# Attention and two feed-forward layers in one kernel: half-column weight loads, a rewritten opening order, and products of zeros

## The chip, the cores and the metric

The kernel runs on one core of a Trainium2 chip. A core has a matrix engine (TensorE, PE in the rows, its weight loads PEld), a vector engine (VectorE, DVE), a scalar engine (ScalarE, ACT), a general engine (GpSimd, POOL), and a queue engine that issues the transfers here (SyncE, SP). Each executes its own instructions in order. The metric is the device time of one execution in microseconds.

## The reference, cut to what matters

```
x = causal_attention(q, k, v)         # 2 batches x 12 heads, 448 tokens, width 64 -> 896 x 768
h = ((x @ w1) * (x @ w2)) @ w3        # 768 -> 1024 -> 1024
y = h @ w_out                         # 1024 -> 768
z = relu(y @ w_in2) ** 2 @ w_out2     # 768 -> 2048 -> 768
```

q, k and v are float32. The weights arrive as 8-byte floats. Softmax subtracts the row maximum and divides by the row sum plus 1e-9.

## The kernel before, in words

**Attention and one weight product share the opening.** The 24 heads go in 12 pairs p. While VectorE and ScalarE do softmax, TensorE has time left, and it fills it with the product w3 @ w_out (into `wraw`), so that h @ w_out needs one product less later. That product is cut into 32 units `(g, i, n)`: group g of four w_out tiles, tile i of w3, column half n (384 columns). `fill()` issues none, one or two units at a time by a fixed count. The loop has 13 slots; slot p does the softmax of pair p and the values of pair p - 1.

**One pair's work.** `scores(p)`: TensorE, four row blocks (112 to 448 columns wide) for each of two heads, into six PSUM banks. `minima(p)`: VectorE adds the mask and takes the row extremum, block by block, which also frees the six banks. `exps(p, j)`: ScalarE, head j. `divide(p, j)`: two small VectorE instructions that wait for the exponentials, then four multiplications, on GpSimd, or on VectorE for head 1 of pairs 0, 1 and 11. `p_transposes(h)`: ten TensorE transposes into three banks of the same six, and three ScalarE copies out (L277). `attend(p)`: the product with v, into one of two banks that the units use too. `x_parts(p)`: ScalarE and VectorE write the two parts of the result.

**Weights.** A weight tile goes through three stages, in a fixed list `order`. Load (L78): 128 x 768 or 128 x 512 eight-byte words. Decode to float32: ScalarE L102, VectorE L103 and L108. Split into a high and a low part: ScalarE L90, VectorE L106. `step()` decodes the next tile of `order` and splits the next one of `parts`, and issues the loads that come free. At most two decoded tiles outside the plain ones wait for their split (`XB`); with two waiting, a step decodes nothing. The first two w3 tiles and the first four w_out tiles are also used as plain float32 (`PLAIN`): units of w3 tiles 0 and 1 are eight instructions of plain float32, all others twelve of split parts, and those need the split w3 tile and all four split w_out tiles of the group. Each unit is then copied out of its bank (L318, VectorE).

**What sets the order.** Inside `manual_schedule` the instructions of the engines named (TensorE, VectorE, ScalarE) run in the order in which the Python code writes them. Transfers and GpSimd are placed by a planner. An instruction waits for what it reads and for the buffers that it overwrites; the rest of its queue waits behind it. Slots 0 to 3 and 12 have an order of their own, slots 4 to 11 share one. A unit's place against the steps in a slot is thus a matter of the written order. `warm()` issues 36 transposes that nothing uses, ahead of the first real transposes. After the 13 slots come the four big products, in which TensorE is busy throughout.

Slot 3 before, with pair 2's values (steps in the order written):

```
scores(3); step(); minima(3); exps(3, 0); fill(); divide(3, 0)
p_transposes(4); p_transposes(5); step(); exps(3, 1); fill()
attend(2); divide(3, 1); x_parts(2); step(); fill()
```

Of the kernel before, what the change touches and what calls it, by code (L numbers as in the profile page):

```python
# [17 lines left out]
def attention_moe_moe2(ctx: ExitStack, tc: tile.TileContext, qk, v, w1, w2, w3, w_out, w_in2, w_out2, out):  # L18
# [13 lines left out]
    nc = tc.nc  # L32
# [17 lines left out]
    XB = 2  # L50
    RAW = 3
    PLAIN = 2
    WARM = 36
    NEAR = 2
    CLOSE = 4
# [13 lines left out]
        return nc.tensor.matmul(o, l, r, start=start, stop=stop)  # L69


    raws, f32s = {}, {}

    def load(key, src):
        n = src.shape[-1]
        pool, tag = (ringp, "ring") if key in LENT else (rawp, "raw")
        t = pool.tile([P, DM, 2], U32, tag=tag, name=f"raw_{key[0]}_{key[1]}")
        nc.sync.dma_start(out=t[:, :n].rearrange("p f w -> p (f w)"), in_=src.bitcast(U32))  # L78
        raws[key] = t[:, :n]

    def convert(a=None, b=None):

        if b:
            nm, n = b
            if nm == "w3":
                t = w3_tile(n)
            else:
                t = ringp.tile([P, 2, DM], F32R, tag="ring", name=f"hl_{nm}_{n}")
            x = wraw[:, n, :] if nm == "W" else f32s[b] if whole(b) else f32s.pop(b)
            nc.scalar.copy(t[:, 0], x)  # L90
            hls[b] = t
        if a:
            raw = raws.pop(a)
            n = raw.shape[1]
            low, high = raw[:, :, 0], raw[:, :, 1]
            if whole(a) and a[0] == "w3":
                y = w3_tile(a[1])[:, 0].bitcast(F32)
            elif whole(a):
                y = w3p[0].tile([P, DM], F32, tag="xw", name=f"xw_{a[1]}", bufs=NB)
# [4 lines left out]
            f32s[a] = y  # L104
# [28 lines left out]
    for g in range(N3 // KF):  # L133
        for i in range(KF):
            order += [("w3", g * KF + i)]
            if g == 0 and i == 0:
                order += [("wout", f) for f in range(NB)]
            if g == 0 and NB - 1 <= i < 2 * NB - 1:
                order += [("wout", i + 1)]
    order += ring[KF:]  # L140
    source = {"wout": w_out, "w1": w1, "w2": w2, "w3": w3, "win2": w_in2, "wout2": w_out2}
    place = {key: i for i, key in enumerate(order)}
# [36 lines left out]
    with (  # L179
# [2 lines left out]
        tc.tile_pool(name="attc", bufs=1) as attc,  # L182
        tc.tile_pool(name="ps_a", bufs=6, space=PSUM) as ps_a,
    ):
        ident = attc.tile([P, P], F32, tag="ident", name="ident")
        mask = attc.tile([CP, S], F32, tag="mask", name="mask")
        make_identity(nc, ident)
# [7 lines left out]

        def load_pair(p):
            t = attq.tile([P, 2, S], F32, tag="qk", name=f"qk{p}", bufs=3)
            nc.sync.dma_start(out=t.rearrange("p i s -> p (i s)"), in_=qk[p])
# [10 lines left out]
        def scores(p):  # L209

            y = qk_t.pop(p)
            st_t[p] = att.tile([CP, 4, 2, NCH], F32, tag="st", name=f"st{p}", bufs=3)
            ps = {}
            for j in range(2):
                p_t[2 * p + j] = att.tile([CP, off[NCH]], F32, tag="p", name=f"p{p}_{j}", bufs=4)
                for g in BLOCKS:
                    t = ps_a.tile([P, S], F32, tag="a", name=f"s{p}_{j}_{g[0]}")
                    o = 0
                    for i in g:
                        ps[j, i] = t[:CP, o:o + (i + 1) * CP]  # L220
                        o += (i + 1) * CP
            for g in BLOCKS:
                for i in g:
                    w = (i + 1) * CP
                    for j in range(2):
                        own = slice(j * D, (j + 1) * D)
                        mm(ps[j, i], y[own, 0, i * CP:w], y[own, 1, :w], True, True)
            s_t[p] = ps

        def blocks(p, j):  # L230
            return [(i, p_t[2 * p + j][:, off[i]:off[i + 1]]) for g in BLOCKS for i in g]

        def minima(p):

# [22 lines left out]
        def warm():  # L257

            t = ps_w.tile([P, HN], F32, tag="w", name="warm")
            for _ in range(WARM):  # L260
                nc.tensor.transpose(t[:CP, :CP], ident[:CP, :CP], ident[:CP, :CP])

        coff = [0, 4 * CP, 7 * CP, 9 * CP]

# [36 lines left out]
        def w_half(g, i, n):  # L301
# [12 lines left out]
            dst = wraw[:, i, cols]  # L314
            if g > 0:
                nc.vector.tensor_tensor(dst, acc, dst, op=ALU.add)
            else:
                nc.vector.tensor_copy(dst, acc)  # L318

        units = [(g, i, n) for g in range(N3 // KF) for i in range(KF) for n in range(2)]  # L320
        NU = len(units)


        parts = [key for key in order if not (key[0] == "w3" and key[1] < PLAIN)]
        steps = [0, 0]

        def free(key):

            if key[0] == "w3":
                return done[1] >= 2 * (key[1] - 1)  # L330
            k = in_ring.get(key, 0) - RING
            return k < 0 or k < NB and done[1] >= NU // 2

        def ahead(n):

            last = max(order.index(key) for key in LENT)
            return max(n + RAW, min(n + RAW + len(LENT), last + 1 + RAW))

        def step(f32=True, split=True):
            a, b = order[steps[0]], parts[steps[1]]  # L340
# [19 lines left out]
                done[1] += 1  # L360

        ET = mybir.EngineType
        with tc.manual_schedule(engines={ET.PE, ET.DVE, ET.Activation}):
            load_pair(0)
            load_pair(1)
            make_loads(2)
            load_v(0)
            make_loads(RAW)
            for p in range(SLOTS):
                softmax, attn_v = p < NP_ALL, p > 0  # L370
                if CLOSE <= p < NP_ALL:
                    load_v(p)
                    if p + 1 < NP_ALL:
                        load_pair(p + 1)
                    scores(p)
                    minima(p)
                    exps(p, 0)
                    fill()
# [9 lines left out]
                        step()  # L388
                    attend(p - 1)
                    x_parts(p - 1)  # L390
                    continue
                if softmax:
                    if p > 0:
                        load_v(p)
                        if p + 1 < NP_ALL:
                            load_pair(p + 1)
                        if p == 1:
                            make_loads(ahead(0))
                    scores(p)
                if p > 2:  # L400
                    step()
                if softmax:
                    minima(p)
                    if p == 1:
                        divide(0, 1)
                        step(split=False)
                    exps(p, 0)
                    if p < 2:
                        divide(p, 0)
                    if p < 3:  # L410
                        step(split=False)
                fill()
                if softmax and p > 1:
                    divide(p, 0)
                if attn_v:
                    if p == 1:
                        warm()
                    p_transposes(2 * (p - 1))
                    p_transposes(2 * (p - 1) + 1)
                    step(split=p > 1)  # L420
                if softmax:
                    exps(p, 1)
                fill()
                if p == 2:
                    step()
                if attn_v:
                    attend(p - 1)
                    if softmax and p > 1:
                        divide(p, 1)
                    x_parts(p - 1)  # L430
                    for _ in range(2 if p == 2 else 1):
                        step(split=p > 1)
                    if p == 1:
                        divide(1, 1)
                fill()
        assert not units and all(k in hls for k in ring[:KF])
        made.update(f32=steps[0], hl=steps[1] + PLAIN)
        for f in range(KF):
            used(("wout", f))

# [172 lines left out]
```

## Time and profile before

| what | us |
|---|---|
| median of 3 runs | 577.47 (577.46 to 577.71) |
| the profiled execution | 577.6 |
| its span, first to last instruction | 575.4 |
| TensorE busy in the span | 563.9 |
| TensorE's first product starts | 4.07 |
| end of the 13 slots (first product of the next stage) | 163.22 |

Times in rows count from the start of the span. The profiled execution is 2.2 us longer than its span, for what lies around it. A TensorE instruction's duration includes its way through the array, so neighbours overlap; from start to start is what one costs in a stream. The same holds for ScalarE and VectorE rows, whose successor often starts before the row's end.

### The profile page before, as it was taken

Reading aid. Unit: us, or ns where it says so; the run is one execution under the profiler, and the core shown is the slowest. Engines: PE = TensorE matmul, PEld = TensorE weight load, DVE = VectorE, ACT = ScalarE, POOL = GpSimd, SP = SyncE. Lnnn points to the kernel's source line nnn. Section 1 sums busy time; section 2 is a strip of 40 time slices with the busy share of each in tenths; the row PEclk is TensorE's granted clock in tenths of the full one; section 3 lists DMA queues with packets and bytes.
Section 4 is the critical chain, followed back from the end, with each engine's and each line's share of the span. In section 5 each row is a group of like instructions: output and inputs, shape, how many; then the busy total and the mean of one; then the engine's idle time right before and its main releaser. Section 6 shows DMA issues by size and latency. Waiting matters only on the chain.

```text
span 575.4 us, 8129 instructions
## 1 busy us (share of the span) xinstructions
PE 563.9 (98%) x3144; PEld 506.5 (88%) x3144; DVE 281.3 (49%) x567; ACT 268.2 (47%) x574; POOL 159.1 (28%) x140
## 2 busy tenths in 40 slices
PE   7899999999999999999999999999999999999997
PEld 5557777778989999999999999999999999999997
DVE  5987887767687544222210484555102854421011
ACT  5778777757865533222210456666002666640000
POOL 3367677776200312111100003333000023330000
PEclk9999999999999999999999999999999999999999
DMA  8854554233266633000000274333100763000111
GB/s 318 288 194 140 177 159 159 84 124 120 88 225 245 204 120 107 9 1 1 1 1 0 67 271 156 109 111 110 56 1 4 270 219 110 1 1 29 56 55 56
DMA packets 14823, 63.96 MB, mean 111 GB/s; under 512 B 1665, under 2 KB 1921, under 8 KB 14785
## 3 DMA queue, kind: packets, MB, share of 16 engines
q1 hardware_dynamic: 14784, 63.45, 32.2%
q8 instruction: 25, 0.41, 0.3%
q14 instruction: 14, 0.11, 0.1%
HBM read 60.69 MB, written 2.75 MB: 110 GB/s over the span
## 4 chain that ended last, share of the span: by engine, by line
PE 86%; DVE 6%; ACT 5%; issue 1%; DMA 1%; DVEq 0%; ACTq 0%
PE w L69 28%; PE g L69 20%; PE o L69 20%; PE h L69 10%; PE s L69 3%; PE x L69 2%; PE pp L273 2%; ACT p L245 2%; ACT pt L277 2%; DVE p L238 1%; DVE xw L108 1%; DMA qk<-in_qk 1%; ACT hl_wout L90 1%; DVE raw_wout L103 0%; DVE x_wout L108 0%
## 5 line engine op out<-in xcount | busy, mean ns | idle before, releaser
L69 PE MATMUL g<-hT,hl_win 128*128 128x448 f32 x576 | 117.2, 365 | 0.0
L69 PE MATMUL w<-xT,hl_w 128*128 128x448 f32 x576 | 117.0, 365 | 0.0
L69 PE MATMUL o<-hl_wout,gT 128*128 128x384 f32 x672 | 116.9, 334 | 0.0
L69 PEld LDWEIGHTS o<-hl_wout,gT 128*128 128x128 f32 x672 | 116.6, 188 | 0.1
L69 PEld LDWEIGHTS g<-hT,hl_win 128*128 128x128 f32 x576 | 108.1, 188 | 8.5
L69 PEld LDWEIGHTS w<-xT,hl_w 128*128 128x128 f32 x576 | 108.1, 188 | 8.5
L255 POOL TENSOR_SCALAR p<-p,st 112x448 f32<-112x448 f32 (+1 forms) x84 | 96.5, 1166 | 51.9 <-DVE st L252 23.3
L120 POOL TENSOR_TENSOR gT<-r,gT 128x448 fp32r<-128x448 f32 x32 | 39.1, 1245 | 195.8 <-ACT gT L119 128.7
L69 PE MATMUL w<-hl_wout,w 128*128 128x384 f32 x336 | 64.4, 342 | 0.5 <-DVE w L106 0.3
L245 ACT ACTIVATE p<-p,st 112x448 f32<-112x448 f32 (+1 forms) x96 | 49.7, 530 | 27.1 <-DVE st L238 27.0
L69 PEld LDWEIGHTS w<-hl_wout,w 128*128 128x128 f32 x336 | 57.4, 188 | 3.9 <-issue 0.9
L69 PE MATMUL h<-abT,hl_W 128*128 128x448 f32 x288 | 58.5, 365 | 0.0
L69 PEld LDWEIGHTS h<-abT,hl_W 128*128 128x128 f32 x288 | 54.1, 188 | 4.3
L120 POOL TENSOR_TENSOR abT<-a,abT 128x448 fp32r<-128x448 f32 x16 | 21.8, 1377 | 111.8 <-ACT abT L119 111.8
L238 DVE CUSTOM_DVE_ANT_0 p<-s,mask 112x448 f32<-112x448 f32 (+1 forms) x96 | 36.5, 441 | 7.0 <-PE s L69 7.0
L106 DVE TENSOR_TENSOR hl_wout<-x_wout,hl_wout 128x768 fp32r<-128x768 f32 x20 | 19.1, 957 | 37.9 <-ACT hl_wout L90 37.9
L533 ACT ACTIVATE r<-g 128x448 f32<-128x448 f32 x32 | 15.8, 542 | 40.8 <-PE g L69 40.8
L69 PE MATMUL s<-qk 64*112 64x448 f32 (+3 forms) x192 | 28.6, 443 | 4.1 <-DMA qk<-in_qk 4.1
L560 DVE TENSOR_TENSOR acc<-o,acc 128x384 f32<-128x384 f32 x14 | 7.2, 553 | 49.0 <-PE o L69 49.0
L273 PE MATMUL pp<-ident,p 112*112 112x112 f32 x240 | 27.9, 262 | 3.3 <-DVE st L238 1.6
L102 ACT ACTIVATE x_w<-raw_w 128x768 f32<-128x768 f32 (+1 forms) x30 | 24.4, 815 | 13.7 <-DVE hl_w L106 10.9
L273 PEld LDWEIGHTS pp<-ident,p 112*112 112x112 f32 x240 | 23.5, 134 | 8.0 <-issue 2.8
(62 smaller groups left out, 538.0 us busy)
## 6 DMA issues: line engine op xcount, KB each, us to landing
raw_wout<-in_w_out SPq DMA_DIRECT2D x24, 768.0 KB, 4.5
raw_w<-in_w SPq DMA_DIRECT2D x16, 768.0 KB, 4.3
raw_win<-in_w_in SPq DMA_DIRECT2D x16, 768.0 KB, 4.2
raw_w<-in_w SPq DMA_DIRECT2D x16, 512.0 KB, 3.9
qk<-in_qk SPq DMA_DIRECT2D x12, 448.0 KB, 5.1
v<-in_v SPq DMA_DIRECT2D x12, 224.0 KB, 2.6
out<-acc SPq DMA_DIRECT2D x6, 384.0 KB, 2.3
out<-acc SPq DMA_DIRECT2D x2, 192.0 KB, 1.8
```

What stands on the lines that cost most here:

```text
L69: return nc.tensor.matmul(o, l, r, start=start, stop=stop)
L90: nc.scalar.copy(t[:, 0], x)
L102: nc.scalar.activation(y, high.bitcast(F32), AF.Prelu, scale=2.0 ** -112, alpha=-2.0 ** 32)
L106: nc.vector.tensor_tensor(t[:, 1], x, t[:, 0].bitcast(F32), op=ALU.subtract)
L120: (engine or nc.vector).tensor_tensor(lo, x, hi.bitcast(F32), op=ALU.subtract)
L238: nc.vector.tensor_tensor_reduce(e, ps[j, i], mask[:, S - (i + 1) * CP:], QS, 3.0e38, ALU.add, ALU.min, st_t[p][:, 0, j, i:i + 1],)
L245: nc.scalar.activation(e, e, AF.Exp, bias=st_t[p][:, 0, j, i:i + 1], scale=-1.0, accum_out=st_t[p][:, 1, j, i:i + 1])
L255: engine.tensor_scalar(e, e, st[:, 3, i:i + 1], None, ALU.mult)
L273: nc.tensor.transpose(x[:CP, o:o + CP], pt[:, off[i] + c * CP:off[i] + (c + 1) * CP], ident[:CP, :CP],)
L277: nc.scalar.copy(t[:, coff[g[0]]:coff[g[0]] + o], x[:CP, :o])
L533: nc.scalar.activation(r, o[b], AF.Relu)
L560: nc.vector.tensor_tensor(a, o[n], a, op=ALU.add)
```

## The change

1. The first four w_out tiles are loaded and decoded in two column halves each: order now begins w3 0, w_out 0 to 3 (left half), w3 1, w_out 0 to 3 (right half), w3 2, w3 3, w3 4, w_out 4, w3 5, w_out 5 and so on. Units 1 and 2 change places, so that the first two units, (0, 0, 0) and (0, 1, 0), read left halves alone.
2. The four units of plain float32 are copied out by ScalarE (L318) in place of VectorE.
3. Slots 0 to 3 are written in another order, with four more steps in all; pair 0's blocks go from small to large, and its q and k come in two halves. Slots 4 to 12 keep their order. The transfers of the opening are issued in the written order too (SP joins the engines named).
4. TensorE begins with 8 products of a 112 x 112 tile of zeros (`warm_zeros`), which nothing uses. `warm()` stays.

Slot 3 after: `scores(3); step(); minima(3); exps(3, 0); fill(); divide(3, 0); p_transposes(4); p_transposes(5); step(); step(); exps(3, 1); fill(); attend(2); divide(3, 1); x_parts(2); step(); step(); fill()`.

```diff
+    WARM0 = 8
...
     def load(key, src):
-        n = src.shape[-1]
-        pool, tag = (ringp, "ring") if key in LENT else (rawp, "raw")
-        t = pool.tile([P, DM, 2], U32, tag=tag, name=f"raw_{key[0]}_{key[1]}")
-        nc.sync.dma_start(out=t[:, :n].rearrange("p f w -> p (f w)"), in_=src.bitcast(U32))
-        raws[key] = t[:, :n]
+        whole_key = key[:2]
+        if whole_key not in raw_t:
+            pool, tag = (ringp, "ring") if whole_key in LENT else (rawp, "raw")
+            raw_t[whole_key] = pool.tile([P, DM, 2], U32, tag=tag, name=f"raw_{key[0]}_{key[1]}")
+        cols = columns(key, src.shape[-1])
+        t = raw_t[whole_key][:, cols]
+        nc.sync.dma_start(out=t.rearrange("p f w -> p (f w)"),
+                          in_=src.bitcast(U32)[:, 2 * cols.start:2 * cols.stop])
+        raws[key] = t
+
+    def columns(key, n):
+
+        return slice(key[2] * n // 2, (key[2] + 1) * n // 2) if key[2:] else slice(0, n)
...
-            if g == 0 and i == 0:
-                order += [("wout", f) for f in range(NB)]
-            if g == 0 and NB - 1 <= i < 2 * NB - 1:
-                order += [("wout", i + 1)]
+            if g == 0 and i < 2:
+                order += [("wout", f, i) for f in range(NB)]
+            if g == 0 and NB <= i < 2 * NB:
+                order += [("wout", i)]
...
+        zeros = attc.tile([CP, CP], F32, tag="xw", name="zeros", bufs=NB)
+        nc.vector.memset(zeros, 0.0)
...
+            if p == 0:
+                x = qk[p].rearrange("p (i s) -> p i s", i=2)
+                for half in (slice(0, S // 2), slice(S // 2, S)):
+                    nc.sync.dma_start(out=t[:, :, half], in_=x[:, :, half])
...
-            for g in BLOCKS:
+            for g in BLOCKS if p else BLOCKS[::-1]:
...
+        def warm_zeros():
+
+            t = ps_w.tile([P, HN], F32, tag="w", name="warm0")
+            for _ in range(WARM0):
+                mm(t[:CP, :CP], zeros, zeros, True, True)
...
+            elif n3 < PLAIN:
+                nc.scalar.copy(dst, acc)
             else:
                 nc.vector.tensor_copy(dst, acc)
...
+        units[1], units[2] = units[2], units[1]
...
-        with tc.manual_schedule(engines={ET.PE, ET.DVE, ET.Activation}):
+        with tc.manual_schedule(engines={ET.PE, ET.DVE, ET.Activation, ET.SP}):
...
+                elif p == 1:
+                    minima(1)
+                    divide(0, 1)
+                    step(split=False)
+                    exps(1, 0)
+                    divide(1, 0)
+                    step(split=False)
+                    fill()
+                    warm()
+                    p_transposes(0)
+                    p_transposes(1)
+                    step(split=False)
+                    exps(1, 1)
+                    fill()
+                    attend(0)
+                    x_parts(0)
+                    step(split=False)
+                    divide(1, 1)
+                    fill()
+                elif p == 2:
+                    minima(2)
+                    exps(2, 0)
+                    divide(2, 0)
+                    step(split=False)
+                    fill()
+                    step(split=False)
+                    step(split=False)
+                    p_transposes(2)
+                    p_transposes(3)
+                    step(split=False)
+                    step(split=False)
+                    exps(2, 1)
+                    fill()
+                    attend(1)
+                    divide(2, 1)
+                    x_parts(1)
+                    step()
+                    step()
+                    fill()
...
+                    p_transposes(2 * (p - 1))
+                    p_transposes(2 * (p - 1) + 1)
+                    for _ in range(2 if p < CLOSE else 1):
+                        step()
+                    if softmax:
+                        exps(p, 1)
+                    fill()
```

## Rows read from the trace of the kernel before

**Rows 1.** The page, busy time and 40 slices of the granted clock (tenths).

```profile
PE 563.9 (98%) x3144; PEld 506.5 (88%) x3144; DVE 281.3 (49%) x567; ACT 268.2 (47%) x574; POOL 159.1 (28%) x140
...
PEclk9999999999999999999999999999999999999999
```

**Rows 2.** Busy time, 11 to 15 us: PE, PEld, DVE, ACT, POOL; granted clock.

```profile
11.00:15.00 4.00, 4.00 (x43) 3.89 (x42) 3.97 (x19) 4.00 (x16) 3.60 (x4) 1.00 1.01 413
```

**Rows 3.** Timeline of TensorE: start, length, what, count, idle before and its releaser.

```profile
4.07 7.07 PE L69 MATMUL s<-qk 64*112 64x448 f32 x32 [4.07 <-DMA qk<-in_qk]
...
14.57 1.16 PE L273 MATMUL pp<-ident,p 112*112 112x112 f32 x10
...
25.93 2.82 PE L273 MATMUL pp<-ident,p 112*112 112x112 f32 x20 [1.24 <-DVE st L238]
...
33.58 2.85 PE L69 MATMUL w<-xw,w 128*128 128x384 f32 x8 [0.20 <-DVE wraw L318]
36.35 2.15 PE L69 MATMUL s<-qk 64*112 64x448 f32 x16
...
41.12 2.81 PE L273 MATMUL pp<-ident,p 112*112 112x112 f32 x20
43.70 2.35 PE L69 MATMUL w<-hl_wout,w 128*128 128x384 f32 x12
45.98 2.11 PE L69 MATMUL x<-pt,v 112*64 112x448 f32 x16
48.31 2.36 PE L69 MATMUL w<-hl_wout,w 128*128 128x384 f32 x12 [0.23 <-DVE wraw L318]
```

**Rows 4.** Score products by width, 4 to 8.3 us: count, busy, mean ns.

```profile
L69 PE MATMUL s<-qk 64*112 64x336 f32 x4 | 1.3, 764 | 0.0
```

**Rows 5.** The same, 9.9 to 10.3 us.

```profile
L69 PE MATMUL s<-qk 64*112 64x336 f32 x4 | 1.1, 660 | 0.0
```

**Rows 6.** The same, 19.5 to 21.7 us.

```profile
L69 PE MATMUL s<-qk 64*112 64x336 f32 x4 | 0.7, 442 | 0.0
```

**Rows 7.** Timeline of VectorE and ScalarE, 8 to 30 us.

```profile
9.90 0.65 ACT L245 ACTIVATE p<-p,st 112x448 f32<-112x448 f32 x1
...
11.95 0.92 ACT L102 ACTIVATE xw<-raw_wout 128x768 f32<-128x768 f32 x1
...
16.29 0.56 DVE L103 TENSOR_SCALAR raw_wout<-raw_wout 128x768 uint32<-128x768 uint32 x1
16.95 0.96 DVE L108 SCALAR_TENSOR_TENSOR xw<-xw,raw_wout 128x768 uint32<-128x768 uint32 x1
...
27.88 0.67 ACT L102 ACTIVATE w<-raw_w 128x512 f32<-128x512 f32 x1
...
28.11 0.42 DVE L103 TENSOR_SCALAR raw_w<-raw_w 128x512 uint32<-128x512 uint32 x1
...
28.46 2.27 ACT L277 COPY pt<-pp 112x448 f32<-112x448 f32 x6
...
28.64 0.69 DVE L108 SCALAR_TENSOR_TENSOR w<-w,raw_w 128x512 uint32<-128x512 uint32 x1
29.25 0.55 DVE L318 COPY wraw<-w 128x384 f32<-128x384 f32 x1
```

**Rows 8.** Timeline of VectorE and ScalarE, slot 3.

```profile
35.70 1.58 ACT L90 CAST hl_wout<-xw 128x768 fp32r<-128x768 f32 x2
...
37.16 0.64 ACT L90 CAST w<-x_w 128x512 fp32r<-128x512 f32 x1
37.27 2.08 DVE L106 TENSOR_TENSOR hl_wout<-xw,hl_wout 128x768 fp32r<-128x768 f32 x2
...
40.34 0.61 DVE L238 CUSTOM_DVE_ANT_0 p<-s,mask 112x448 f32<-112x448 f32 x1
...
43.06 2.29 ACT L277 COPY pt<-pp 112x448 f32<-112x448 f32 x6
```

**Rows 9.** Busy time of slot 7, columns as in rows 2.

```profile
92.02:102.45 10.43, 10.43 (x78) 8.27 (x77) 7.33 (x27) 8.37 (x26) 6.88 (x7) 1.00 0.49 168
```

More of the change, by code (lines that the diff above doesn't have):

```diff
@@ L69, in mm @@
         return nc.tensor.matmul(o, l, r, start=start, stop=stop)
-    raws, f32s = {}, {}
+    raw_t, raws, f32s = {}, {}, {}
     def load(key, src):
-        n = src.shape[-1]
-        pool, tag = (ringp, "ring") if key in LENT else (rawp, "raw")
-        t = pool.tile([P, DM, 2], U32, tag=tag, name=f"raw_{key[0]}_{key[1]}")
-        nc.sync.dma_start(out=t[:, :n].rearrange("p f w -> p (f w)"), in_=src.bitcast(U32))
-        raws[key] = t[:, :n]
+        whole_key = key[:2]
[9 more added lines that the diff above has]
+        return slice(key[2] * n // 2, (key[2] + 1) * n // 2) if key[2:] else slice(0, n)
     def convert(a=None, b=None):
@@ L98, in convert @@
             elif whole(a):
-                y = w3p[0].tile([P, DM], F32, tag="xw", name=f"xw_{a[1]}", bufs=NB)
+                if a[:2] not in f32s:
+                    f32s[a[:2]] = w3p[0].tile([P, DM], F32, tag="xw", name=f"xw_{a[1]}", bufs=NB)
+                y = f32s[a[:2]][:, columns(a, DM)]
             else:
@@ L103, in convert @@
             nc.vector.tensor_scalar(low, low, 2.0 ** -29, 7.0, ALU.mult, ALU.min)
-            f32s[a] = y
+            f32s.setdefault(a[:2], y)
         if b:
@@ L197, in load_pair @@
             t = attq.tile([P, 2, S], F32, tag="qk", name=f"qk{p}", bufs=3)
-            nc.sync.dma_start(out=t.rearrange("p i s -> p (i s)"), in_=qk[p])
+            if p == 0:
+                x = qk[p].rearrange("p (i s) -> p i s", i=2)
+                for half in (slice(0, S // 2), slice(S // 2, S)):
+                    nc.sync.dma_start(out=t[:, :, half], in_=x[:, :, half])
+            else:
+                nc.sync.dma_start(out=t.rearrange("p i s -> p (i s)"), in_=qk[p])
             qk_t[p] = t
@@ L221, in scores @@
                         o += (i + 1) * CP
-            for g in BLOCKS:
+            for g in BLOCKS if p else BLOCKS[::-1]:
                 for i in g:
@@ L230, in blocks @@
         def blocks(p, j):
-            return [(i, p_t[2 * p + j][:, off[i]:off[i + 1]]) for g in BLOCKS for i in g]
+            return [(i, p_t[2 * p + j][:, off[i]:off[i + 1]]) for g in (BLOCKS if p else BLOCKS[::-1]) for i in g]
         def minima(p):
@@ L320, in attention_moe_moe2 @@
         units = [(g, i, n) for g in range(N3 // KF) for i in range(KF) for n in range(2)]
+        units[1], units[2] = units[2], units[1]
         NU = len(units)
-        parts = [key for key in order if not (key[0] == "w3" and key[1] < PLAIN)]
+        parts = [key[:2] for key in order if not (key[0] == "w3" and key[1] < PLAIN) and key[2:] != (1,)]
         steps = [0, 0]
@@ L329, in free @@
             if key[0] == "w3":
-                return done[1] >= 2 * (key[1] - 1)
+                return done[1] >= 2 * (key[1] - 1) + (key[1] == PLAIN)
             k = in_ring.get(key, 0) - RING
@@ L334, in ahead @@
         def ahead(n):
-            last = max(order.index(key) for key in LENT)
-            return max(n + RAW, min(n + RAW + len(LENT), last + 1 + RAW))
+            last = {key[:2]: i for i, key in enumerate(order)}
+            places = []
+            for i, key in enumerate(order):
+                if key[0] == "W":
+                    return i
+                if key[:2] not in LENT and key[:2] not in places:
+                    if len(places) >= RAW and last[places[-RAW]] >= n:
+                        return i
+                    places.append(key[:2])
         def step(f32=True, split=True):
@@ L367, in attention_moe_moe2 @@
             load_v(0)
-            make_loads(RAW)
+            make_loads(1 + NB)
+            load_pair(2)
+            load_v(1)
+            make_loads(ahead(0))
+            warm_zeros()
             for p in range(SLOTS):
                 softmax, attn_v = p < NP_ALL, p > 0
-                if CLOSE <= p < NP_ALL:
+                if p > 1 and softmax:
                     load_v(p)
@@ L374, in attention_moe_moe2 @@
                         load_pair(p + 1)
+                if softmax:
                     scores(p)
+                if p == 0:
+                    minima(0)
+                    exps(0, 0)
+                    divide(0, 0)
+                    step(split=False)
+                    exps(0, 1)
+                    for _ in range(GAPS):
+                        fill()
[29 more added lines that the diff above has]
+                    step(split=False)
+                    step(split=False)
+                    exps(2, 1)
[6 more added lines that the diff above has]
+                    fill()
+                elif CLOSE <= p < NP_ALL:
                     minima(p)
@@ L390, in attention_moe_moe2 @@
                     x_parts(p - 1)
[L391 to L400, printed above, removed]
-                    step()
[L402 to L408, printed above, removed]
-                        divide(p, 0)
-                    if p < 3:
-                        step(split=False)
@@ L412, in attention_moe_moe2 @@
[L412 to L417, printed above, removed]
+                else:
+                    step()
+                    if softmax:
+                        minima(p)
+                        exps(p, 0)
+                    fill()
+                    if softmax:
+                        divide(p, 0)
                     p_transposes(2 * (p - 1))
                     p_transposes(2 * (p - 1) + 1)
-                    step(split=p > 1)
@@ L421, in attention_moe_moe2 @@
[L421 to L426, printed above, removed]
+                    for _ in range(2 if p < CLOSE else 1):
+                        step()
+                    if softmax:
+                        exps(p, 1)
+                    fill()
                     attend(p - 1)
-                    if softmax and p > 1:
+                    if softmax:
                         divide(p, 1)
@@ L430, in attention_moe_moe2 @@
                     x_parts(p - 1)
[L431 to L435, printed above, removed]
+                    for _ in range(2 if p < CLOSE else 1):
+                        step()
+                    fill()
         assert not units and all(k in hls for k in ring[:KF])
-        made.update(f32=steps[0], hl=steps[1] + PLAIN)
+        made.update(f32=steps[0], hl=place[parts[steps[1]]])
```

## The prediction

> **What bounds the kernel now.** The page comes first: TensorE is busy 98% of the span, the others half or less [rows 1]. From 163 us on it never waits in any row, and nothing of the change reaches there except by the time at which that stage starts. So the question is when the thirteenth slot ends (163.2 us now), and the timeline of TensorE's opening is the view to read [rows 3]. Look there for three losses: 4.07 us before the first product; products at half rate; and waits, the longest 1.24 us, at the transposes of slot 2. The busy times say why there are waits: from 11 to 15 us VectorE, ScalarE and TensorE are all full [rows 2]. Until about 45 us three queues run neck and neck, and an instruction moved from one to another only helps if the receiving one has room at that place.
>
> The clock row shows full speed throughout [rows 1], but the products' own rows don't: a 336-column score product averages 764 ns from 4 us on [rows 4], 660 just at 9.9 us [rows 5] and 442 in slot 2 [rows 6]. The difference, 322 ns, is close to two passes of 336 columns at 1.2 against 2.4 GHz (280 ns). So TensorE was at the lower level from its first product at 4.07 to about 9.85 us, 5.8 us, which cost up to 2.9 us.
>
> **The way of counting.** I put each engine's instructions one after another in the written order, each with the start-to-start time of its rows and no earlier than what it reads. Slots of the kernel before, put together so, give unit 4 at 43.5 us (43.70 in rows 3) and the end of the slots at 163.3 (163.2). The unit times are: four exponentials 2.05 us (9.90 to 11.95), decoding a 512-wide tile 0.57 on ScalarE (27.88 to 28.46) and 0.42 + 0.72 on VectorE, six copies of transposes 2.27 [rows 7]; splitting a 768-wide tile 0.73 on ScalarE (two in 1.46) and 0.95 to 1.0 on VectorE [rows 8].
>
> **Part 1, the front.** The products of zeros, 16 instructions of two passes of 112 columns, take 3.0 us at the lower clock, and run from about 0.95 to 3.95 us, where TensorE has nothing else. The first half of q and k can't land before about 3.3 us (the whole lands at 4.02 with 448 KB; half is 224 KB less, 0.65 us at the 340 GB/s of the opening), so the scores start at about 3.95, 0.1 us earlier. If the zeros raise the clock as the first products did, 5.8 us after they begin, it rises at 6.7 us: the scores of pairs 0 and 1, 16 instructions each, save about 1.1 us. Bounds: no rise by zeros, 0.65 us less than I take; a rise before the scores, 1.0 us more. The first transposes then come at 13.4 where they came at 14.57: minus 1.2 us.
>
> **Part 2, the halves.** VectorE's decoding of a whole w_out tile is 0.56 + 0.96 [rows 7]. A half is not half: between 768 and 512 columns the two instructions lose 0.41 us, so 384 columns cost about 0.94 in place of 1.52. Four left halves save 2.3 us on VectorE before the minima of slot 2, of which some 1.1 us go in waiting for the values of pair 0. With minima(0) 0.95 us earlier, minima(2) start 2.2 us earlier, and the transposes of slot 2 behind them at 23.5 to 23.9 in place of 25.93 [rows 3]. So far a gain of 2.0 to 2.4 us. The added price is four decodings more: 4 x 0.36 us on VectorE and under 0.1 each on ScalarE, all in slot 2.
>
> **Part 3, slot 2.** Here ScalarE becomes the chain. From the first minimum (23.45) it has, in order: four exponentials 2.05, decode w3 1 0.57, copy of unit 0 0.48, two right halves 0.92, copies of transposes 2.27, two right halves 0.92, four exponentials 2.05, copy of unit 1 0.48: 9.7 us, so 33.2 to 33.4. (The copy's price on ScalarE isn't in the trace; 0.38, the mean copy of transposes, and 0.55, VectorE's, bound it [rows 7]. I take 0.48.) Unit 2 needs the bank that unit 1's copy frees, so it starts at 33.4, against 33.58 before [rows 3]. Before, the same stretch of ScalarE had neither right halves nor copies, and VectorE freed the bank. Scores of pair 3: 36.05 against 36.35. Of the 2 us only 0.3 are left.
>
> **Part 4, slot 3, where it turns.** Unit 4 is the first of split parts: it needs the split of w_out 0 to 3 and of w3 2. Before, the first step of slot 3 finished these, ahead of the minima; TensorE went from the transposes to unit 4 without a wait (41.12 + 2.6 = 43.70 [rows 3]). In the new order slot 2 splits two w_out tiles in place of four; slot 3 splits w_out 2 in its first step, and w_out 3 and w3 2 in the two steps written behind the transposes, just ahead of unit 4. On ScalarE these casts stand behind the six copies, which stand behind the transposes, exps(3, 0) and unit 3's copy. VectorE before it: after x_parts(1), at 34.3, it has two steps of 0.42 + 0.95 + 0.72 and a split of 0.95, 5.1 us, so minima(3) start at 39.5 (40.34 before [rows 8]). ScalarE: exponentials 40.05 to 42.1, copy 42.6, transposes' copies 44.95 (before, they ran from 43.06 to 45.3 [rows 8]), cast of w_out 3 and of w3 2 to 46.3. TensorE ended its transposes at 42.75 and stands 3.6 us; then two products, and 0.7 us for the low part of w3 2 on VectorE (47.3). Unit 4 ends at 49.2 in place of 45.98 [rows 3]: plus 3.2 us. Queued behind it are attend(2), unit 5 and the scores of pair 4. Of this 0.2 us come back, since unit 5 no longer waits its 0.23 [rows 3]: plus 3.0 at slot 4. Bounds: 2.0 (ScalarE 1 us earlier) and 4.
>
> **Part 5, slots 4 to 12.** Their order is unchanged. But one split fewer is done by slot 4 (six against seven), since a step decodes nothing while two tiles wait. The leftover shifts through slots 4 to 6, and falls into slots 7 and 8 ahead of their minima. Slot 7 had no wait in 10.43 us, with VectorE busy 7.33 [rows 9]. Price between 0 (it fits into those 3.1 us) and 2.1 us (a 512-wide decode 1.14 and a split 0.95, in full); I take 1.0, as minima, on which the transposes wait, come right behind.
>
> The sum: 577.6 + 3.0 + 1.0 = 581.6 on the profiled execution; the median shown is 0.1 us lower, so 581.5.
>
> **Rivals.** (a) The clock falls again. Before, no wait of TensorE after 4.07 us is over 1.24 us [rows 3], and rows 6 show the upper level; a stand of 3.6 us at unit 4 is new. If it falls, it is the opening once more: 5.8 us at the lower level, 2.9 us lost at most, less where others are late anyway: 584.4. The Trainium skill's page "TensorE: Matmul & The Clock Gate", section "HAM oscillation — how this bites in real kernels", describes exactly this: waits between bursts that bring the clock back down each time. No row here shows a fall, so I leave it a rival, at 0.2. (b) Faster. ScalarE frees the bank of unit 1 early enough, and the 2 us of the front reach slot 3. Then the transposes end at 40.7, the casts behind their last copy (0.4) end at 42.4, and unit 4 starts before 43.7; it decides at about 2.6 us: that much earlier must ScalarE be at the cast of w_out 3 than the 44.95 of part 4. With it, and with the clock up at once, the gain is 1 to 2 us: 576.0. For it speaks that 5% on ScalarE's times is 0.5 us of the 9.7; against it that the casts can't precede the transposes in any case. 0.11. (c) The halves don't do what they say: if the reader of a left half waited for the right half of its tile too, slot 1's decodings would wait for transfers at 17.6 to 21 us, and 1 us is added: 582.6. Against it: pair 0's first exponentials read one block while others of the same tile are still being written. 0.05. (d) No change: part 4's wait at its lower end and no part 5, with the clock up at once: 577.6 + 2.0 - 0.2 - 1.0 = 578.4. 0.05.
>
> **How the numbers follow.** Main case 0.59 with a range of its own of 579.8 to 583.2 (bounds of parts 1, 4 and 5 together); (a) 0.2, (b) 0.11, (c) 0.05, (d) 0.05. What a measurement can tell from no change is about 0.2%, 1.2 us. Faster: (b) 0.11. Same: (d) and a little, 0.06. Slower: the rest, 0.83. The range runs from 579.0, which leaves (b) and (d) out, to 584.8, which takes (a) in.
>
> **What would show it.** Unit 4 right behind the two casts on ScalarE, with TensorE idle 3 to 4 us ahead of it; that is the step on which the sign rests. The first score products at about 4 us, the change of their duration near 6.7 us. Transposes of slot 2 at 23.5 to 24 us; unit 2 released by ScalarE's copy near 33.4. Products of slot 3 and 4 at the upper level (rival (a) if not). The last unit ending near 167.5 us. If unit 4 starts before 44 us, parts 3 and 4 are wrong; if it stands and the end is still early, part 5 or the front is.

## The result

Slower: 583.4 us median (583.07 to 583.87, four runs) where the kernel before takes 577.56 (577.46 to 577.71, four runs beside them). The ratio is 1.0101, interval 1.0086 to 1.0116. The profiled execution took 583.63 us with a span of 581.8, so what lies around the span is 1.8 us where it was 2.2.

The page first (busy time, and the granted clock in 40 slices of 14.5 us):

```profile
PE 569.1 (98%) x3160; PEld 510.4 (88%) x3160; DVE 281.5 (48%) x572; ACT 270.2 (46%) x582; POOL 161.2 (28%) x140
...
PEclk9998999999999999999999999999999999999999
```

TensorE is still busy 98% of the span, with 5.2 us more of it than in [rows 1]. Only 16 instructions were added, the products of zeros, and they take 3.3. Some of the rest must have run slower, and slice 4 of the clock, an 8, says about where. The timeline of TensorE's opening is the same view as [rows 3]:

```profile
1.03 3.33 PE L70 MATMUL warm<-zeros 112*112 112x112 f32 x16 [1.03 <-DVE zeros L197]
4.29 6.12 PE L70 MATMUL s<-qk 64*112 64x112 f32 x32
10.34 3.66 PE L279 MATMUL warm<-ident 112*112 112x112 f32 x36
...
24.24 2.82 PE L297 MATMUL pp<-ident,p 112*112 112x112 f32 x20 [0.40 <-DVE st L256]
28.32 2.82 PE L70 MATMUL w<-xw,w 128*128 128x384 f32 x8 [1.26 <-DVE w L119]
31.07 2.11 PE L70 MATMUL x<-pt,v 112*64 112x448 f32 x16
33.67 2.85 PE L70 MATMUL w<-xw,w 128*128 128x384 f32 x8 [0.49 <-ACT wraw L342]
36.45 2.15 PE L70 MATMUL s<-qk 64*112 64x448 f32 x16
38.53 2.85 PE L70 MATMUL w<-xw,w 128*128 128x384 f32 x8
41.21 2.08 PE L297 MATMUL pp<-ident,p 112*112 112x112 f32 x20
46.16 0.62 PE L70 MATMUL w<-hl_wout,w 128*128 128x384 f32 x2 [2.87 <-ACT w L99]
47.28 3.52 PE L70 MATMUL w<-hl_wout,w 128*128 128x384 f32 x10 [0.51 <-DVE w L117]
...
55.08 2.15 PE L70 MATMUL s<-qk 64*112 64x448 f32 x16
```

Read the starts against [rows 3]. At slot 2's transposes the new kernel is 1.7 us ahead (24.24 against 25.93). At the scores of pair 3 it is 0.1 behind (36.45 against 36.35): the lead is gone, most of it in two waits of TensorE, 1.26 us for VectorE ahead of unit 1 and 0.49 for ScalarE ahead of unit 2. Then unit 4, the first unit of split parts, starts at 46.16 in place of 43.70, and its last ten products take 3.52 us where all twelve took 2.35 before. The scores of pair 4 are 4.5 us late (55.08 against 50.60). The next stage is 5.9 us late: its first two products, which the view groups apart, start at 168.98 against 163.08 (the others at 169.12; the table has 163.22). Behind that the kernels are alike: the last addition on VectorE starts 409.03 us after those two products in both.

ScalarE and VectorE of slot 3 say what unit 4 waited for, as [rows 8] do for before:

```profile
39.46 0.61 DVE L256 CUSTOM_DVE_ANT_0 p<-s,mask 112x448 f32<-112x448 f32 x1
...
42.19 0.46 ACT L342 COPY wraw<-w 128x384 f32<-128x384 f32 x1
42.55 2.31 ACT L301 COPY pt<-pp 112x448 f32<-112x448 f32 x6
44.72 0.87 ACT L99 CAST hl_wout<-xw 128x768 fp32r<-128x768 f32 x1
45.45 0.65 ACT L99 CAST w<-x_w 128x512 fp32r<-128x512 f32 x1
...
46.55 0.68 DVE L117 TENSOR_TENSOR w<-x_w,w 128x512 fp32r<-128x512 f32 x1
```

The two casts stand behind the six copies of the transposes. Unit 4's first two products follow the second cast, the other ten the end of VectorE's split. The stretch around unit 4 gives the clock (start and end, length and busy time of PE, PEld, DVE, ACT, POOL; granted clock; DMA share, GB/s):

```profile
46.50:47.00 0.50, 0.28 (x2) 0.00 (x0) 0.50 (x2) 0.50 (x3) 0.50 (x1) 1.00 0.00 0
47.00:47.50 0.50, 0.22 (x1) 0.22 (x2) 0.23 (x1) 0.50 (x4) 0.50 (x1) 0.71 0.00 0
47.50:50.50 3.00, 3.00 (x10) 2.84 (x10) 0.00 (x0) 0.66 (x4) 0.36 (x1) 0.50 0.00 0
50.50:51.00 0.50, 0.50 (x4) 0.20 (x4) 0.16 (x1) 0.00 (x0) 0.00 (x0) 0.88 0.00 0
51.00:52.00 1.00, 1.00 (x8) 0.43 (x6) 0.65 (x3) 0.00 (x0) 0.12 (x1) 1.00 0.00 0
```

From about 47.2 to 50.6 us TensorE had 0.50, the 1.2 GHz level. The record turns to 0.50 after a stand of 2.87 us and about 1 us in which two products ran and TensorE paused for 0.5.

### The profile page after: what moved, and what is told of

It is laid out like the page before. It is cut to its first block, busy times and chain, and to the rows that moved or that the text cites. A ratio compares the mean times of both kernels' runs of the same rounds, so it can differ in the third digit from the quotient of the medians.

```text
span 581.8 us, 8181 instructions
## 1 busy us (share of the span) xinstructions
PE 569.1 (98%) x3160; PEld 510.4 (88%) x3160; DVE 281.5 (48%) x572; ACT 270.2 (46%) x582; POOL 161.2 (28%) x140
## 4 chain that ended last, share of the span: by engine, by line
PE 84%; ACT 8%; DVE 4%; issue 2%; DMA 1%; SPq 0%; DVEq 0%; ACTq 0%
PE w L70 28%; PE g L70 20%; PE o L70 20%; PE h L70 10%; ACT p L263 4%; PE x L70 2%; ACT pt L301 2%; PE pp L297 2%; PE s L70 2%; DMA raw_w<-in_w 1%; DVE p L256 1%; ACT xw L113 1%; DVE xT L131 1%; DVE x_w L119 0%; ACT hl_wout L99 0%
## 5 line engine op out<-in xcount | busy, mean ns | idle before, releaser
L273 POOL TENSOR_SCALAR p<-p,st 112x112 f32<-112x112 f32 (+2 forms) x84 | 98.3, 1186 | 56.0 <-DVE st L270 29.6
L70 PE MATMUL w<-hl_wout,w 128*128 128x384 f32 x336 | 66.7, 349 | 4.1 <-ACT w L99 2.9
L70 PEld LDWEIGHTS w<-hl_wout,w 128*128 128x128 f32 x336 | 58.6, 192 | 8.5 <-ACT w L99 3.5
L263 ACT ACTIVATE p<-p,st 112x112 f32<-112x112 f32 (+2 forms) x96 | 49.9, 533 | 24.9 <-DVE st L256 24.9
L256 DVE CUSTOM_DVE_ANT_0 p<-s,mask 112x112 f32<-112x112 f32 (+2 forms) x96 | 36.5, 444 | 5.3 <-PE s L70 5.3
L117 DVE TENSOR_TENSOR hl_wout<-x_wout,hl_wout 128x768 fp32r<-128x768 f32 x20 | 19.1, 957 | 36.5 <-ACT hl_wout L99 36.5
L119 DVE SCALAR_TENSOR_TENSOR x_wout<-x_wout,raw_wout 128x768 uint32<-128x768 uint32 x20 | 25.8, 1288 | 5.1 <-ACT x_wout L113 4.9
```

The source lines that it names most:

```text
L119: nc.vector.scalar_tensor_tensor(y.bitcast(U32), y.bitcast(U32), 3, low, op0=ALU.logical_shift_left, op1=ALU.bitwise_or)
L256: nc.vector.tensor_tensor_reduce(e, ps[j, i], mask[:, S - (i + 1) * CP:], QS, 3.0e38, ALU.add, ALU.min, st_t[p][:, 0, j, i:i + 1],)
L263: nc.scalar.activation(e, e, AF.Exp, bias=st_t[p][:, 0, j, i:i + 1], scale=-1.0, accum_out=st_t[p][:, 1, j, i:i + 1])
L273: engine.tensor_scalar(e, e, st[:, 3, i:i + 1], None, ALU.mult)
```

## The experiments

My theory: two costs at unit 4, the place of the casts (about 2.5 us) and the clock that falls because of it (about 1.7), and a third in slots 4 to 12 (1.4). Rivals: ScalarE's copies, the new front, or a stand that costs nothing of the clock. The medians of before beside these runs were 577.40 to 577.45 us. Starts are those of the profiled executions, one of each kernel.

**1. The casts ahead of the transposes.** In slot 3 of the changed kernel the two steps behind the transposes join the first one, so that three come ahead of the minima; the two at the end stay.

```diff
-                    step()
+                    for _ in range(3 if p == 3 else 1):
+                        step()
                     if softmax:
                         minima(p)
...
-                    for _ in range(2 if p < CLOSE else 1):
+                    for _ in range(0 if p == 3 else 1):
                         step()
                     if softmax:
                         exps(p, 1)
```

> The changed kernel with the two steps behind slot 3's transposes moved ahead of minima(3); everything else as changed. Theory (the place of these two steps makes the wait at unit 4, and the wait makes the fall of the clock): unit 4 follows the transposes without a wait, the clock row stays full, minima(3) start some 2 us later (41.6), and the kernel takes about 579.3 us, 4 us less than the changed one (583.4). Rival (ScalarE is late in any order, because it copies units and decodes halves): the wait moves in front of unit 4's neighbours, and 582.5 or more remains.

Measured: 579.18 us (578.95 to 581.02), ratio 1.0038 (1.0025 to 1.0051).

```profile
41.27 2.82 PE L297 MATMUL pp<-ident,p 112*112 112x112 f32 x20 [0.49 <-DVE st L256]
43.86 2.35 PE L70 MATMUL w<-hl_wout,w 128*128 128x384 f32 x12
...
50.48 2.15 PE L70 MATMUL s<-qk 64*112 64x448 f32 x16
```

Unit 4 follows the transposes without a wait, the clock stays in the profile, and 4.2 us of the median are gone. From the scores of pair 3 to those of pair 4 it takes 14.63 us, the changed kernel 18.63, the kernel before 14.25. So the place of the casts, with the clock, costs 4.0 us, and 0.4 stay in this kernel too, which now waits 0.49 us at the transposes for minima behind three steps. At the scores of pair 4 it is 0.1 us ahead of before, but only because this trace had a luckier opening (scores of pair 3 at 35.85, with the same text up to there; see experiment 5). Its next stage starts 1.2 us later than before (164.25 against 163.08), and its median is 1.7 above: the third cost remains. In the highest of its five runs the mean clock was 0.996, in the others 0.998 to 1.0; no trace shows where that one lost it.

**2. TensorE kept busy.** The stand stays, but products that nothing uses fill it.

```diff
+            if (n3, n) == (2, 0):
+                t = ps_w.tile([P, HN], F32, tag="w", name="busy")
+                for _ in range(14):
+                    mm(t[:CP, :CP], ident[:CP, :CP], ident[:CP, :CP], True, True)
             acc = ps_w.tile([P, HN], F32, tag="w", name=f"w{n3}_{n}")
```

> The changed kernel with 14 products of the identity (28 instructions, 2.6 us at full clock) that nothing uses, written ahead of unit 4, where TensorE stands still for 2.9 us. Theory (the stand itself costs about 2.5 us, and the fall of the clock behind it another 1.7): unit 4 starts at the same 46.2 us, but at full clock, and the kernel takes 581.7 us. Rival (the fall of the clock is hidden behind waits of other engines): 583.4, no change. If the added products came too late to be free, it would be slower.

Measured: 582.39 us (582.11 to 582.79), ratio 1.0088 (1.0072 to 1.0105).

```profile
43.23 2.92 PE L70 MATMUL busy<-ident 112*112 112x112 f32 x28
46.24 0.62 PE L70 MATMUL w<-hl_wout,w 128*128 128x384 f32 x2
47.37 2.01 PE L70 MATMUL w<-hl_wout,w 128*128 128x384 f32 x10 [0.51 <-DVE w L117]
...
53.66 2.15 PE L70 MATMUL s<-qk 64*112 64x448 f32 x16
```

The time lies between the 581.7 us expected and the rival's 583.4. Unit 4 comes as late as without the filling, but its last ten products take 2.01 us in place of 3.52, and the next stage starts 1.51 us earlier (167.47 against 168.98). That is the price of the clock in these two traces. The mean granted clock is 0.999 to 1.0 in all four runs, against 0.997 in all four of the changed kernel. The medians differ by only 1.0 us; the profiled executions, 582.11 and 583.63, by 1.5.

**3 and 4. The plain units' copies.** In the changed kernel VectorE copies again; in the kernel before ScalarE copies.

```diff
# 3: the changed kernel
-            elif n3 < PLAIN:
-                nc.scalar.copy(dst, acc)
# 4: the kernel before
+            elif n3 < PLAIN:
+                nc.scalar.copy(dst, acc)
```

> The changed kernel with the four plain units copied by VectorE again, as before. Theory (the steps' place decides, the copies only shift work between two full queues): unit 2 starts about 1 us earlier, minima(3) 1 to 1.5 us later, unit 4 still waits for the casts; 583.4 to 584. Rival (the copies on ScalarE are what takes the front's 2 us away): 581.5 or less.

> The kernel before with the four plain units copied by ScalarE (L318), nothing else. Theory (ScalarE is as full as VectorE there, and a copy behind exponentials frees the bank late): unit 2 starts 1.4 us later, and about 1 us is left at the end: 578.5. Rival (VectorE is the tighter queue, and 2 us less on it help): 576.5 to 577.5.

Measured: 583.24 us (582.68 to 585.48), ratio 1.0108 (1.0088 to 1.0128), and 577.77 us (577.47 to 578.01), 1.0007 (0.9998 to 1.0016). In kernel 3 unit 2 starts at 33.52 without a wait (33.67 with ScalarE's copy), but unit 4 at 46.17: nothing is won. (This trace's slot 2 began 0.3 us later, at 24.56 against 24.24; counted from there, unit 2 comes 0.5 us earlier and unit 4 0.3, which the times don't show.) In kernel 4 there is a wait of 1.51 us for ScalarE's copy, and it hardly costs anything, where 578.5 us were expected:

```profile
34.67 2.85 PE L69 MATMUL w<-xw,w 128*128 128x384 f32 x8 [1.51 <-ACT wraw L318]
...
42.21 2.08 PE L273 MATMUL pp<-ident,p 112*112 112x112 f32 x20
44.06 2.34 PE L69 MATMUL w<-hl_wout,w 128*128 128x384 f32 x12
```

Unit 2 is 1.1 us late, but the transposes of slot 3 take 1.85 us to the next unit in place of 2.58, which fits banks that the minima had freed by then, and the scores of pair 4 are 0.2 us late (50.82 against 50.60). The copies are no cause that the times show.

**5. The changed kernel without the products of zeros.**

```diff
-    WARM0 = 8
+    WARM0 = 0
...
-        zeros = attc.tile([CP, CP], F32, tag="xw", name="zeros", bufs=NB)
-        nc.vector.memset(zeros, 0.0)
...
+            if not WARM0:
+                return
```

> The changed kernel without the tile of zeros and its 8 products. Theory (they raise the clock earlier): the score products stay at the lower clock until 9 to 10 us, the first transposes come 0.4 to 1 us later, and 583.8 to 584.2 us. Rival (products of zeros don't count, or later waits hide the difference): 583.4, or a little less as the scores start with their first half.

Measured: 583.98 us (583.91 to 584.78), ratio 1.0117 (1.0102 to 1.0132). The scores start 0.5 us earlier, at 3.79, and end 0.7 later: the 36 transposes of `warm()` begin at 11.07 against 10.34. By the medians the zeros earn about 0.6 us, less than the intervals can tell apart.

A pair of traces can't price them either, for one and the same opening differs from run to run. Kernel 8 below opens like the kernel before, yet its 448-column products had reached full speed where those of before were still slow. Before (8.2 to 8.6 us), then kernel 8 (7.9 to 8.2):

```profile
L69 PE MATMUL s<-qk 64*112 64x448 f32 x2 | 1.0, 951 | 0.0
```

```profile
L69 PE MATMUL s<-qk 64*112 64x448 f32 x4 | 0.9, 536 | 0.0
```

Read so, by the products' durations, the clock rose between 5.4 and 7.1 us in the seven traces with zeros, and between 7.4 and 10.2 in the four without. In the five traces with zeros and the changed order `warm()` begins between 9.91 and 10.74 us. So the products of zeros do bring the rise forward, though their operands are zeros; but starts of two traces tell nothing finer than some 0.8 us if they are not counted from a common point behind the opening.

**6 and 7. The front alone.** The kernel before with the zeros, pair 0's halves and its blocks from small to large (6), and with pair 2's q and k loaded ahead of w_out 2 and 3 besides (7).

```diff
+            load_pair(2)
             warm_zeros()
...
-                        if p + 1 < NP_ALL:
+                        if p > 1 and p + 1 < NP_ALL:
```

> The kernel before with three things of the change alone: the 8 products of zeros, q and k of pair 0 in two halves, and pair 0's blocks from small to large. No halves of w_out, no copies on ScalarE, no other order in slots 1 to 3. Theory (the front is a gain of its own, which slots 2 and 3 lost): the transposes of slot 2 come 0.9 us earlier, and since slot 3 keeps its order most of it stays: 576.6 us. Rival (waits further on take it back): 577.5, no change.

> The kernel of the run with the front alone, with q and k of pair 2 loaded ahead of w_out 2 and 3 in place of behind them. There, the scores of pair 2 waited 1.36 us for this transfer (20.4 us), which took the front's gain back. Theory: without it the scores of pair 2 start at 19.0 us, the transposes of slot 2 at 24.5 to 24.8, and slot 3 keeps its order, so that 0.7 to 0.9 us are left at the end: 576.6 us, about 0.15% under the kernel before. Rival (w_out 3 lands later by as much and the first unit waits for its decode instead): 577.2, as with the front alone.

Measured: 577.21 us (576.49 to 578.15, eleven runs), ratio 0.9999 (0.999 to 1.0008), and 577.64 us (577.14 to 578.93, eleven runs), 1.0007 (0.9998 to 1.0015). Kernel 6, then kernel 7:

```profile
14.07 2.69 PE L287 MATMUL pp<-ident,p 112*112 112x112 f32 x20
...
20.41 2.15 PE L70 MATMUL s<-qk 64*112 64x448 f32 x16 [1.36 <-DMA qk<-in_qk]
...
25.37 2.82 PE L287 MATMUL pp<-ident,p 112*112 112x112 f32 x20
```

```profile
19.31 2.15 PE L70 MATMUL s<-qk 64*112 64x448 f32 x16
21.39 3.16 PE L70 MATMUL w<-xw,w 128*128 128x384 f32 x8
25.79 2.82 PE L287 MATMUL pp<-ident,p 112*112 112x112 f32 x20 [1.24 <-DVE st L246]
```

Both were expected at 576.6 us. In kernel 6 the scores of pair 2 wait 1.36 us for their transfer and come 0.8 us later than before, but this costs nothing: the transposes of slot 2 depend on the minima on VectorE, which start at 24.60 us in place of 25.16, and come 0.6 us earlier. That lead is still 0.5 us at the scores of pair 4 (50.09 against 50.60) and at the next stage (162.56 against 163.08), and the profiled execution is 0.5 us shorter. In kernel 7 the transfer is early, but the minima start at 25.02, and the transposes wait 1.24 us for them, as in [rows 3]: VectorE, which still decodes whole tiles, sets the pace there in any case. The medians don't confirm the half microsecond: by the interval of kernel 6, a front that is earlier alone earns at most 0.1%, 0.6 us.

**8. The kernel before with its split late.** The same cause from the other side: slot 3's first step moves behind the transposes, and nothing else changes.

```diff
-                if p > 2:
+                if p > 2 and p != 3:
                     step()
                 if softmax:
                     minima(p)
...
-                    step(split=p > 1)
+                    for _ in range(2 if p == 3 else 1):
+                        step(split=p > 1)
                 if softmax:
                     exps(p, 1)
```

> The kernel before with slot 3's first step (it splits w3 2) moved from ahead of minima(3) to behind the transposes, beside the step that is there; nothing else. Theory (a cast written behind the copies of transposes makes unit 4 wait): TensorE waits some 2.3 us ahead of unit 4, more than 1.24 and less than the changed kernel's, 1.5 us are left at the end (579.0), and whether the clock falls with it is open (then 580 to 581). Rival (the place of a step doesn't matter as ScalarE has room): 577.5.

Measured: 580.22 us (578.91 to 580.63), ratio 1.0046 (1.0032 to 1.0059).

```profile
40.76 2.20 PE L273 MATMUL pp<-ident,p 112*112 112x112 f32 x20
44.95 4.06 PE L69 MATMUL w<-hl_wout,w 128*128 128x384 f32 x12 [1.99 <-ACT w L90]
...
53.28 2.15 PE L69 MATMUL s<-qk 64*112 64x448 f32 x16
```

```profile
45.00:48.30 3.30, 3.30 (x10) 2.87 (x11) 2.84 (x4) 2.86 (x9) 3.30 (x3) 0.50 0.00 0
```

One step moved makes unit 4 wait 1.99 us for ScalarE, and the twelve products behind it take 4.06 us: the clock (second view) was at 0.50 here too, as soon as unit 4 began. By the mean clock it fell in three of the four runs (0.996 to 0.997, 580.21 to 580.63 us). The fourth, of which there is no trace, kept 1.0 and took 578.91. If its stand was as long, that is the stand alone, 1.5 us above before, and the fall adds 1.3 to 1.7.

**9. One step more in slot 4.** Kernel 1 with a step moved from the end of slot 5 to slot 4, behind the transposes, so that the leftover split is made up there.

```diff
-                    step()
+                    for _ in range(2 if p == 4 else 1):
+                        step()
                     exps(p, 1)
...
-                    for _ in range(2 if p < 7 or p % 2 == 0 else 1):
+                    for _ in range(1 if p == 5 else 2 if p < 7 or p % 2 == 0 else 1):
```

> The kernel of the run with slot 3's steps ahead (579.2), with one step moved from the end of slot 5 to slot 4, behind its transposes; nothing else. There, slots 7 and 8 were 1.1 us longer than before with their transposes held by the minima, and slot 3 ended with one split fewer than before. Theory (the leftover split travels down the slots until it meets the minima of 7 and 8): made up in slot 4, at the price of 0.5 us there, it gives slots 6 to 8 about 1.5 us back: 578.1 us. Rival (the longer slots 7 and 8 come of something else, as the transfers in written order): 579.2 or more.

Measured: 579.11 us (578.46 to 580.39), ratio 1.0033 (1.0021 to 1.0046): no different from kernel 1, and not the 578.1 expected. From the scores of pair 4 to the next stage it takes 113.24 us where kernel 1 takes 113.77 and the kernel before 112.48. So 0.5 us came back; of this nothing shows in the time, since in this trace the scores of pair 4 came 0.8 us later (51.28 against 50.48) after a slower opening. Slots 7 and 8 stayed long: 11.16 and 13.01 us, against 10.43 and 12.51 before. The leftover split had not gone, though. Counted on VectorE, kernel 9 has begun 12 splits by the start of slot 6, as many as the kernel before (the changed one has 11). But slot 6 begins two where it begins three in the other kernels counted, and at slot 7 the counts are 14 in kernel 9, in kernel 1 and in the changed kernel, and 15 before. So kernel 9 doesn't test what slots 7 and 8 cost without the leftover.

## Why the prediction was right, and where it was off

The sign, its cause and its place were right: slower, by a stand at unit 4, on which parts 3 and 4 rested. The median of 583.4 lies inside the range, 1.9 us above the 581.5 forecast. It lies inside only because the range takes in rival (a): the main case's own bounds end at 583.2.

**Part 1 and part 2, the front.** The scores began at 4.29 in place of 3.95, for the zeros take 3.26 us in place of 3.0 and start at 1.03, not 0.95. By the durations of the 336-column products the clock rose between 6.1 and 6.5 us (6.7 forecast). That it came so close is in part luck. The 5.8 us at the lower level were read from one trace, a little short (in it two products that start at 9.43 us still take 764 and 831 ns, so the rise came at about 10.2, after 6.1 us), and in kernel 8, with the same opening, it came at about 7.4 us. Slot 2's transposes came at 24.24 (23.5 to 23.9): a gain of 1.7, not 2.0 to 2.4. One wait was not foreseen: unit 1 stood 1.26 us for VectorE's decoding of w3 1, which follows minima(2).

**Part 3, slot 2.** Unit 2 came at 33.67 (33.4), released by ScalarE's copy as said. But that copy is not alone: with VectorE copying (kernel 3), unit 2 starts only 0.5 us earlier, counted from the transposes of slot 2, since unit 1 behind VectorE's decoding and the values of pair 1 behind it are nearly as late. Two queues end there almost together.

**Part 4, where it turns.** Minima(3) at 39.46 (39.5), the cast of w_out 3 at 44.72 (44.95), unit 4 at 46.16 (46.3), the low part 1.1 us behind it (1.0). TensorE stood 2.87 us there, not 3.6, for its transposes ended at 43.3, not 42.75. Kernels 1 and 8 show the cause from both sides: with the casts ahead of the transposes the stand is gone, and with one step behind them the kernel before has one.

**The step that failed is the main case's clock**, which was left at the upper level. Rival (a), with a chance of 0.2, is what happened; it was priced at 2.9 us, after the opening's 5.8 us at the lower level. Kernel 2 measures 1.5, for the lower level lasted only from about 47.2 to 50.6 us here. The sentence "No row here shows a fall, so I leave it a rival" took a lack of long stands for evidence: the rows of before had none over 1.24 us after the opening, so they could say nothing about one of 3. In the trace of after the clock reads 0.50 behind the stand, and kernel 2 without the stand has 1.00 there. The Trainium skill's page "TensorE: Matmul & The Clock Gate", section "HAM oscillation — how this bites in real kernels", tells of waits between bursts that bring the clock down, in its kernel waits of about 3 to 5 us. The trace agrees that a stand does, and shows it after one of 2.87 us, shorter than those.

**Part 5, slots 4 to 12.** Priced at 1.0, between 0 and 2.1, it measured 1.42: 112.48 us before, 113.90 after, from the scores of pair 4 to the next stage. The kernels with before's order (4, 6, 7, 8) have 112.42 to 112.47, those with the new one 113.56 to 113.81 (kernels 1, 2, 3, 5). Of the place, slots 7 and 8 were right: they hold 1.15 of it. Slot 7, to set beside [rows 9]:

```profile
96.77:107.85 11.08, 10.94 (x78) 8.29 (x76) 8.87 (x28) 8.66 (x26) 7.82 (x7) 1.00 0.49 158
```

VectorE is busy 8.87 us where it was 7.33: 1.0 us more of splits (L117: 1.89, from 0.89) and 1.0 more of the second instruction of decodings (L119: 2.06, from 1.05), less 0.5 in the rest. The first minimum comes 3.40 us after the slot's scores in place of 2.20, and the transposes, which need the banks, take 2.71 in place of 2.08. So the leftover does fall into slot 7 ahead of its minima, as forecast: every changed kernel whose splits were counted (the changed one, 1 and 9) starts slot 7 one split behind, at 14, and begins two splits in it, where the kernel before and kernel 8 have 15 and one. That slots 7 and 8 are longer for this alone is not shown: no run removes it, kernel 9 included, and none separates it from the transfers in written order.

**The sum**, with what was measured: the scores of pair 4 come 4.5 us late, of which the clock is 1.5. The other 3.0 are as forecast: 2.5 for the casts' place, 0.4 that kernel 1 keeps too, and 0.1 that was lost by the scores of pair 3. Slots 4 to 12 add 1.4; together 5.9. The time grew by 6.0 in the profiled executions.

## What to carry to other kernels

Before a step is moved, ask not only what its queue has room for, but which work the moved instruction will stand behind: two casts that take 1.4 us cost 2.5, and 1.5 more by the clock, because they came to stand behind copies that stand behind the very transposes after which their reader is written. When a forecast makes the matrix engine stand longer than any stand in the trace, price the clock as part of the main case. And time won at the front is worth only what the next queues can take: the changed kernel was 1.7 us ahead at the transposes of slot 2, and had lost it in waits for VectorE and ScalarE by the scores of pair 3.

## What the runs showed of the hardware

- A stand of 1.99 us was followed by a fall of the clock in three runs of four (kernel 8), one of 2.87 with a second of 0.5 in all four of the changed kernel (mean clock 0.997), and, by the mean clock of 0.994 to 0.997, stands of 2.72 and 2.86 in all four runs of kernels 3 and 5. With the same stand filled by identity products (kernel 2) none showed a fall (0.999 to 1.0).
- After shorter stands none was seen in a trace: 1.51 us in kernel 4 (0.999 to 1.0 in all ten runs), 1.24 before (0.999 to 1.0 in all 45 runs beside the experiments). Yet single runs of kernels 1, 6 and 9, whose traces have no stand over 1.4 us, had a mean clock of 0.996 to 0.997. In kernels 1 and 9 that run took 1.8 and 1.3 us more than the median; where the clock fell is not known.
- The fall has no fixed place behind the stand. It appears in the rows as unit 4 begins in kernel 8, 1.0 us later in the changed kernel (within the pause of 0.5), and 1.5 and 2.0 us later in kernels 3 and 5, with TensorE at work again.
- At the start the clock row reads 1.00 while products run at half speed: in the changed kernel 336-column products that start at 5.55 us take 764 ns and those at 6.11 some 515, against 442 in slot 2 of before [rows 6]. There the products' own durations tell the level, and the row doesn't.
